# Attention beside a dense network: row maxima kept in queues of their own, more of them ahead of the loop, and slots joined in pairs

## The chip, the cores and the metric

The kernel runs on one core of one Trainium2 chip. The time is the device time of one execution in microseconds (us); several executions give a median and a span of values. One more execution is taken with the hardware profiler, and every instruction time below is from there.

## The reference

```python
xn = layernorm(x)                            # x: 2048 x 512, float32
qkv = xn @ wqkv                              # 32 heads of 16
p = softmax(q @ k.T * 16 ** -0.5)            # per head, 2048 x 2048
s = (p @ v) @ wo
h = relu(xn @ w1 + b1) ** 2                  # 2048 x 1792
g = silu(h @ w2 + b2)
out = x + s * g
```

All of it is float32. Products that need it are made from a high and a low part, three matmuls for one (`terms3`).

## The kernel before, in words

**Units and slots.** Attention is cut into 32 *units*: four heads (a *quad*) and 512 queries each, eight quads with four units. A unit has 16 *slots*, one for each block of 128 keys; there are 512 slots, numbered by `st`. In a slot four score matmuls with the keys on the output's partitions are made (`exp_mm`, L1125), one for each head, 64 rows of the array by 512 columns; ScalarE takes the exponential of each (L1132) into an SBUF tile. Two slots later four matmuls add these tiles, times V, to the unit's sums (`pv_mm`, L362, called a *PV* here; each shows as two records, so a PV is eight).

**Maxima.** The softmax needs the row maxima of a unit before its first slot. They come from score matmuls the other way round, queries on the partitions (`max_mm`, L289), 64 for each unit, 2048 in all, each followed by a VectorE reduction (L296). `max_mm(g, j)` serves unit `g // 16`; `g` is the slot plus `LEAD` = 24, so a unit's maxima end nine slots ahead of it. 24 such steps, 96 maxima, run ahead of the loop. `max_end` (L300) issues loads of K and Q at fixed steps of a unit and reduces the unit's maxima at its end; `shift` (L324) transposes and negates them and sends them through DRAM into two rows of the Q tile.

**Lanes and steps.** The array is split into two row tiles of 64, two *lanes*, that work at once. A *step* is one matmul on each lane. The scores of heads 0 and 2 of a quad and half of their maxima are on lane 0, the others on lane 1. The dense network and the output projection (WO) are cut in halves the same way: each accumulation first runs its upper half of rows on lane 0, later its lower half on lane 1, into the one dense bank (`pd`).

**Slots with dense work.** `slot` puts dense matmuls on one lane (six, or nine and twelve in WO's part), and four exponentials and three or four maxima on the other, in an order written as a string of `s` and `m`. `long_slots` (L1207) takes a *block* of 12 dense pieces for both lanes and spreads it over four slots, that is over two *visits* of two slots: in the first, lane 0 has the dense pieces, in the second, lane 1. A visit has ten steps (`D` ten times beside `msmsmsmsms`), a PV, four steps (`DDss` beside `mmsm`), a PV. The relus that empty a block's bank (`post`) are issued after the second of these four steps. The first dense matmul of a lane has a written dependency on `last_use`, an instruction that reads a score of the other lane (L209, L243); `long_slots` sets it to the exponential of the lane's first `s` of the part `DDss`.

**What sets the order.** TensorE, ScalarE, VectorE, GpSimd and SP run in the loop in the order in which the program is written. `later(n, fn)` runs something n slots on, at `begin`.

**Banks.** Eight PSUM banks: three for exponentials (`pe`), three for maxima (`pm`), one dense (`pd`), one for PV (`pv`). Tiles of a pool are taken in turn, and a matmul waits until the tile's last reader is done.

**Ahead of the loop.** After the layer norm `pump(n)` emits n matmuls of the projections to Q, K and V (twelve for each tile). 83 of them come alone, then the 24 lead steps of two maxima, eight projections, two maxima, eight projections; the last twelve fall into the loop's slots 0 and 1.

Of the kernel before, what the change touches and what calls it, by code (L numbers as in the profile page):

```python
# [8 lines left out]
F32 = mybir.dt.float32  # L9
# [7 lines left out]
P = 128  # L17
# [10 lines left out]
LEAD = 24  # L28
# [3 lines left out]
NPT = 14  # L32
NVT = 7
# [6 lines left out]
def kernel(  # L40
# [55 lines left out]
    with ExitStack() as ph:  # L96
# [8 lines left out]
        turn = {"ka": 0, "qm": 0, "qe": 0, "pt": 0}  # L105
# [6 lines left out]
        def oldest_first(name):  # L112
            n = turn[name] % len(rot[name])
            rot[name] = rot[name][n:] + rot[name][:n]
            turn[name] = 0
# [162 lines left out]
        togo = {}  # L278

        def max_mm(g, j):  # L280
            u = g // 16
            qd = u // 4
            if u not in mxs:
                mxs[u] = sp.tile([P, 16, 4], F32, name="mx")
                for i in range(2):
                    togo[u, i] = [(p, qb, kc) for p in range(2) for qb in range(4) for kc in range(4)]
            p, qb, kc = togo[u, j].pop(0)
            ps = pm.tile([P, 512], F32, name="pm_t")
            nc.tensor.matmul(  # L289
                ps,  # L290
                qms[u][p][64 * j : 64 * j + 64, qb * P : (qb + 1) * P],
                kas[qd, p][64 * j : 64 * j + 64, kc * 512 : (kc + 1) * 512],
                start=True, stop=True,
            )
            c = (2 * p + j) * 4 + qb
            return nc.vector.tensor_reduce(  # L296
                mxs[u][:, c, kc : kc + 1], ps, axis=AX.X, op=ALU.max
            )

        def max_end(g):  # L300
            u, s = divmod(g, 16)
            if u >= NU:
                return
            qd, qc = divmod(u, 4)
            if qc == 2 and qd + 1 < NQ and s % 2 == 0:
                load_k(qd + 1, s // 2)
            if qc == 3 and qd + 1 < NQ and s % 2 == 0 and s < 8:
                load_k(qd + 1, 8 + s // 2)
            if s in (7, 8):
                load_q_pair(u, "qe", s - 7, qes.setdefault(u, []))  # L310
            if s in (9, 11) and u + 1 < NU:
                load_q_pair(u + 1, "qm", (s - 9) // 2, qms.setdefault(u + 1, []))
            if s == 15:
                assert not togo[u, 0] and not togo[u, 1]
                m4 = sp.tile([P, 16], F32, name="m4")
                nc.vector.tensor_reduce(m4, mxs[u], axis=AX.X, op=ALU.max)  # L316
                mxs[u] = m4
                late.append((g + 2, u))

        def shift_due(g):  # L320
            if late and late[0][0] <= g:
                shift(late.pop(0)[1])

        def shift(u):  # L324
            pt = pm.tile([P, 512], F32, name="pm_t")
            nc.tensor.transpose(pt[:16, :P], mxs[u], ident)  # L326
            sh = sp.tile([16, 2, P], F32R, name="sh", bufs=1)
            nc.vector.tensor_scalar(sh[:, 0], pt[:16, :P], -1.0, None, op0=ALU.mult)
            nc.vector.scalar_tensor_tensor(
                sh[:, 1], pt[:16, :P], -1.0, sh[:, 0].bitcast(F32),  # L330
                op0=ALU.mult, op1=ALU.subtract,
            )
            def keep():
                for i in range(2):
                    nc.sync.dma_start(
                        sh_d[u][:, i, :].rearrange("h (b n) -> h b n", n=P),
                        sh[:, i, :].bitcast(F32),
                    )

            def back():  # L340
                for p in range(2):
                    for i in range(2):
                        shift_rows(u, p, i)

            if in_loop:
                later(1, keep)
                later(2, back)
            else:
                keep()
                back()  # L350
# [63 lines left out]
        def mlp_tasks(mp):  # L414
# [127 lines left out]
            def second(c, tt):  # L542
# [30 lines left out]
                if c == NCK - 1 and tt:  # L573

                    for i, task in enumerate(halves(mms, (6,) * 7, post, 1)):
                        if i == 4:
                            oldest_first("pt")
                            rot["pt"][:] = [t for t in rot["pt"] if all(t is not x for x in rot["ex"])]
                        yield task
                    return  # L580
# [19 lines left out]
            for c in range(NCK):  # L600
                if c == 1:

                    oldest_first("pt")
                    rot["pt"][:0] = rot["ex"]
# [307 lines left out]

        def qk_tile(m, c, last=False):
            ps = pd.tile([P, 512], F32, name="pd_t") if last else pe.tile([P, 512], F32, name="se")
# [13 lines left out]
            if m % 4 == 0:  # L928
# [10 lines left out]
        def v_tile(c, tt):  # L939
            xT = xTs[c]  # L940
            ps = pe.tile([P, 512], F32, name="se")
# [12 lines left out]
            nc.sync.dma_start(v_d[:, c * 4 + tt, :], vt.rearrange("p h d -> p (h d)"))  # L954
            yield
# [48 lines left out]
        def pump(n):  # L1004
            for _ in range(n):
                while True:
                    todo = ahead or rest
                    if not todo:
                        return
# [72 lines left out]
        pump(83)  # L1082
        warm = const.tile([P, 1], F32, name="warm")
        nc.scalar.activation(warm, eps_t, AF.Exp)
        for g in range(LEAD):
            shift_due(g)
            for j in range(2):
                max_mm(g, j)
            pump(8)
            for j in range(2):  # L1090
                max_mm(g, j)
            pump(8)
            max_end(g)
            if g == 0:
                raw_r = [load_w("wv", 3 * P, ((D + P, 3 * P),))]
            if g == 3:
# [4 lines left out]
            if g == 12:  # L1101
                s1.close()
                ep = ph.enter_context(tc.tile_pool(name="ep", bufs=1))
                rot["pt"] = [ep.tile([P, 512], F32, name=f"pt{i}") for i in range(NPT)]
                pools["n"] = ph.enter_context(tc.tile_pool(name="np", bufs=1))
            if g == 16:
                load_v(0)
                nc.sync.dma_start(b1_t, b1.rearrange("(fo p) -> p fo", p=P), allow_slow_non_contiguous=True)
                nc.sync.dma_start(b2_t, b2[None, :].to_broadcast([P, D]))
            if g % 2 and g < 16:  # L1110
                c, i = divmod(g // 2, 2)
                nc.sync.dma_start(
                    xn_d[i, :, :, c * 512 : (c + 1) * 512], xTs[c][:, i].bitcast(F32)
                )
        first.close()

        def exp_mm(st, j, pts, spare):
# [12 lines left out]
            pts[j] = ring("pt")  # L1130
            assert all(t is not pts[j] for d in pts_all.values() if d is not pts for t in d.values()), (st, j)
# [4 lines left out]
        def pv_step(st, pts):  # L1136
# [3 lines left out]
            pv_mm(pos[0], u // 4, kb, pts)  # L1140
            if kb == NT - 1:
# [28 lines left out]
        pts_all = pts  # L1170

        def slot(st, mms, post, fill=0):
            g = st + LEAD
# [4 lines left out]
            spare = g >= NU * 16  # L1178
# [13 lines left out]
            for i in range(len(other)):  # L1192
                if i < len(own):
                    own[i]()
                if other[i] is not None:
                    follow = other[i]()
                    if i >= len(own) - 1 and use is None:
# [6 lines left out]
            if not fill:  # L1204
                max_end(g)

        def long_slots(st0, units, post):  # L1207


            g0 = st0 + LEAD  # L1210
# [7 lines left out]

            for h in range(2):
                own, other = units[h], 1 - h  # L1220
                for part, (mine, theirs) in enumerate((("D" * 10, "msmsmsmsms"), ("DDss", "mmsm"))):
                    st = st0 + 2 * h + part
                    if st > st0:
                        begin(st)
                    for i, ops in enumerate(zip(mine, theirs)):
                        for lane in (h, other) if part else (other, h):
                            o = ops[0] if lane == h else ops[1]
                            if o == "D":
                                own.pop(0)()
                            elif o == "m":  # L1230
                                max_mm(g0, lane)
                            else:
                                use = s(lane)
# [4 lines left out]
                    max_end(st + LEAD)  # L1238
                    shift_due(st + 1 + LEAD)
                    pv_step(st - 2, pts.pop(st - 2))  # L1240
            if post is not None:
# [19 lines left out]
        def begin(st):  # L1261
            now[0] = st
            if st % 64 == 48 and st // 64 + 1 < NQ:
                load_v(st // 64 + 1)
            run_waiting()

        done = 0
        for st_ in range(NU * 16):
# [3 lines left out]
            if st_ < 2:  # L1272
                slot(st_, [], None, 6)
                shift_due(st_ + 1 + LEAD)
# [5 lines left out]
            if st_ == 2:  # L1280

                for g in (LEAD, LEAD + 1):
                    max_end(g)
# [9 lines left out]
            shift_due(st_ + 1 + LEAD)  # L1293
# [32 lines left out]
```

## Time and profile before

| | us |
|---|---|
| median of three runs | 1685.78 |
| lowest and highest | 1684.11, 1688.55 |
| profiled execution, first to last instruction | 1684.0 |
| TensorE busy in it | 1655.3 |
| VectorE, ScalarE, GpSimd busy | 1349.0, 1192.2, 525.5 |

For the profiled execution the profile gives the span from first to last instruction and no other time of its own; the three runs around it lie 0.1 to 4.6 us above that span.

How to read it: PE is TensorE's matmuls, PEld its weight loads, DVE is VectorE, ACT ScalarE, POOL GpSimd, SP the engine that issues the DMAs. In a timeline a row has the start, the time that the row covers, the engine, the line and the operation, the tiles, and how many instructions were merged; in brackets stands the idle time ahead of it and what ended that. A matmul row is longer than the spacing of matmuls, since they are pipelined.

### The profile page before, as it was taken

What the parts mean: (1) busy time and instruction counts of PE and PEld (TensorE: products, weight loads), DVE (VectorE), ACT (ScalarE), POOL (GpSimd) and SP (SyncE); (2) the same over time, 40 slices, a digit from 0 to 9 for tenths busy, and PEclk for the clock granted to TensorE, in tenths of its full rate; (3) what the DMA queues carried; (4) which work ended last, traced back from release to release, by engine and by line L of the source; (5) the groups of instructions that cost most, each with busy time, mean ns of one, the idle gap of its engine ahead of it and who ended that gap; (6) DMA issues with size and microseconds to landing.
All of it is one profiled execution on the core that took longest, in us unless ns stands there. A gap on an engine that the chain in (4) does not pass through costs nothing.

```text
span 1684.0 us, 35391 instructions
## 1 busy us (share of the span) xinstructions
PE 1655.3 (98%) x13296; PEld 941.3 (56%) x13296; DVE 1349.0 (80%) x2296; ACT 1192.2 (71%) x2354; POOL 525.5 (31%) x544
## 2 busy tenths in 40 slices
PE   6999999999999999999999999999999999999998
PEld 5766565556545655565466456545655565555533
DVE  6255688888888888888888888888888888887632
ACT  7211477777777777777777777777777777776685
POOL 4335566522212321231133113311221233134333
PEclk9999999999999999999999999999999999999998
DMA  8648566434333333433333334323433352157444
GB/s 282 177 144 268 165 204 186 117 83 141 90 90 92 116 83 99 100 105 78 103 117 85 85 93 142 95 65 105 137 81 83 82 151 57 44 169 228 140 125 134
DMA packets 156723, 208.00 MB, mean 124 GB/s; under 512 B 51272, under 2 KB 71240, under 8 KB 155016
## 3 DMA queue, kind: packets, MB, share of 16 engines
q1 hardware_dynamic: 156552, 205.74, 42.2%
q8 instruction: 105, 1.72, 0.4%
q14 instruction: 66, 0.54, 0.1%
HBM read 149.30 MB, written 56.09 MB: 122 GB/s over the span
## 4 chain that ended last, share of the span: by engine, by line
PE 88%; issue 4%; DMA 3%; POOL 2%; SPq 1%; DVE 1%; ACT 0%; POOLq 0%; ACTq 0%
PE po L362 27%; PE pm_t L289 17%; PE pd_t L236 16%; PE se L1125 12%; PE pd_t L204 6%; PE se L916 5%; PE se L947 3%; POOL ts L740 1%; POOL ts L741 1%; DMA oc<-on_d 0%; PE pm_t L816 0%; PE pm_t L326 0%; DMA xt<-in_A_x_dram 0%; DMA xc<-xn_d 0%; DMA hl<-r_d 0%
## 5 line engine op out<-in xcount | busy, mean ns | idle before, releaser
L296 DVE TENSOR_REDUCE mx<-pm_t 128x1 f32<-128x512 f32 x2048 | 1275.2, 684 | 233.0 <-PE pm_t L289 139.7
L1132 ACT ACTIVATE pt<-se 128x512 f32<-128x512 f32 x1730 | 902.9, 611 | 254.7 <-PE se L1125 221.6
L289 PE MATMUL pm_t<-ka,qm 64*128 64x512 f32 x2048 | 797.1, 423 | 3.9 <-DVE mx L296 3.7
L1125 PE MATMUL se<-qe,ka 64*128 64x512 f32 x2000 | 685.9, 402 | 0.0
L362 PE MATMUL po<-pt,v 128*32 128x512 f32 x3556 | 544.3, 604 | 0.0
L289 PEld LDWEIGHTS pm_t<-ka,qm 64*128 64x128 f32 x2048 | 352.8, 184 | 279.5 <-DVE mx L296 252.2
L1125 PEld LDWEIGHTS se<-qe,ka 64*128 64x128 f32 x2000 | 339.5, 184 | 21.3 <-issue 5.5
L236 PEld LDWEIGHTS pd_t<-xc,w1s 64*128 64x128 f32 x2352 | 292.1, 187 | 82.3 <-issue 82.2
L236 PE MATMUL pd_t<-xc,w1s 64*128 64x256 f32 x2352 | 332.2, 288 | 0.0
L236 PE MATMUL pd_t<-w2t,hT 64*128 64x512 f32 x936 | 259.9, 410 | 0.0
L236 PEld LDWEIGHTS pd_t<-w2t,hT 64*128 64x128 f32 x936 | 156.0, 184 | 71.2 <-issue 65.4
L362 PE MATMUL po<-ex,v 128*32 128x512 f32 x540 | 192.3, 605 | 0.0
L1132 ACT ACTIVATE ex<-se 128x512 f32<-128x512 f32 x270 | 147.5, 614 | 36.6 <-PE se L1125 31.6
L536 POOL TENSOR_TENSOR r<-r 128x512 f32<-128x512 f32 x49 | 50.9, 1040 | 331.3 <-ACT r L533 331.3
L362 PEld LDWEIGHTS po<-pt,v 128*32 128x32 f32 x3556 | 79.9, 108 | 132.3 <-issue 111.6
L555 POOL TENSOR_TENSOR u<-u,b_t 128x512 f32<-128x512 f32 x16 | 20.5, 1284 | 307.5 <-ACT u L554 307.5
L204 PE MATMUL pd_t<-w2t,hT 64*128 64x512 f32 x408 | 105.6, 391 | 0.0
L400 POOL TENSOR_TENSOR ot<-ot,hl 128x512 f32<-128x512 f32 x31 | 39.8, 1284 | 185.5 <-DMA hl<-r_d 134.8
L204 PE MATMUL pd_t<-wot,oc 64*128 64x512 f32 x336 | 90.4, 405 | 2.4 <-DVE m L316 0.8
L204 PEld LDWEIGHTS pd_t<-wot,oc 64*128 64x128 f32 x336 | 58.6, 184 | 49.1 <-DVE mx L296 12.5
L204 PEld LDWEIGHTS pd_t<-w2t,hT 64*128 64x128 f32 x408 | 72.6, 184 | 8.9
L533 ACT ACTIVATE r<-pd_t,b_t 128x256 f32<-128x256 f32 x98 | 41.1, 470 | 50.1 <-PE pd_t L236 50.1
(111 smaller groups left out, 1110.4 us busy)
## 6 DMA issues: line engine op xcount, KB each, us to landing
w1s<-w_d SPq DMA_DIRECT2D x196, 256.0 KB
qm<-q_d SPq DMA_DIRECT2D x384, 32.0 KB
qe<-q_d SPq DMA_DIRECT2D x384, 32.0 KB
ka<-k_d SPq DMA_DIRECT2D x96, 128.0 KB
xn_d<-xT SPq DMA_DIRECT2D x8, 1024.0 KB
k_d<-hl SPq DMA_DIRECT2D x32, 256.0 KB
q_d<-hl SPq DMA_DIRECT2D x32, 256.0 KB
xc<-xn_d SPq DMA_DIRECT2D x16, 512.0 KB
```

What stands on the lines that cost most here:

```text
L204: mm = nc.tensor.matmul(out_, lh(r), rh(r), start=first_ and lane == 0, stop=last_ and lane == 1, skip_group_check=True,)
L236: mm = nc.tensor.matmul(out_, lh(r), rh(r), start=first_ and lane == 0, stop=last_ and lane == 1, skip_group_check=True,)
L289: nc.tensor.matmul(ps, qms[u][p][64 * j : 64 * j + 64, qb * P : (qb + 1) * P], kas[qd, p][64 * j : 64 * j + 64, kc * 512 : (kc + 1) * 512] ...
L296: return nc.vector.tensor_reduce(mxs[u][:, c, kc : kc + 1], ps, axis=AX.X, op=ALU.max)
L362: nc.tensor.matmul(po[32 * j : 32 * j + 32, :], vs[qd][:, (4 * kb + j) * VW : (4 * kb + j) * VW + 32], pts[j], start=(kb == 0), stop=(kb = ...
L400: nc.gpsimd.tensor_tensor(ot, ot, hl[:, 1].bitcast(F32), op=ALU.mult)
L533: nc.scalar.activation(r[:, i], ps[:, i * CW : (i + 1) * CW], AF.Relu, bias=b1_t[:, fo : fo + 1])
L536: nc.gpsimd.tensor_tensor(r, r, r, op=ALU.mult)
L916: nc.tensor.matmul(out_, lh(slice(0, P)), rh(slice(0, P)), start=first_, stop=last_)
L947: nc.tensor.matmul(out_, lh(slice(0, P)), rh(slice(0, P)), start=first_, stop=last_)
L1125: nc.tensor.matmul(se, kas[qd, j // 2][b : b + 64, kb * P : (kb + 1) * P], qes[u][j // 2][b : b + 64, :], start=True, stop=True,)
L1132: return nc.scalar.activation(pts[j], se, AF.Exp, scale=0.25)
```

## The change

- The maxima are two queues, one for each lane (`todo_m`), in the order of units; `max_mm(j)` takes the next of lane j whatever the slot. `m_ready` holds back those whose K is not yet there. `max_end` follows the count of maxima that are done.
- Ahead of the loop 60 projections come alone, then bursts of three pairs of maxima and twelve projections until one projection tile is left: 34 bursts, 204 maxima. In the bursts maxima use the banks of `pm` and `pe` in turn, projections those of `pd` and `pv`. All projections that follow use the copy on ScalarE and the split on GpSimd.
- K of the next quad is loaded in the first six slots of a quad (of quad 1 ahead of the loop), Q for the exponentials one unit ahead; the shift's rows come back 14 slots ahead of the unit.
- Tiles for exponentials come from a list of free ones (`free_pt`), put back after the PV that reads them.
- Slots with over eight dense pieces take a fifth maximum, with over eleven a sixth.
- A visit of `long_slots` is *fused* where enough maxima are ahead (`ahead_m`, with `SHIFT` = 8): one part of 14 steps, with seven maxima in place of eight, and both PVs behind it. Otherwise it runs in two parts as before; here too the order in a step, the place of `post` and the choice of `last_use` are those of the new helper `visit`.

```diff
+        def ahead_m(n, st):
+            wo0 = 16 * NU - 62
+            for u in range(n // 64, NU):
+                end = 16 * u - SHIFT
+                n_max = n + 4 * max(0, end - st)
+                n_max += max(0, min(end, wo0 + 32) - max(st, wo0))
+                if n_max < 64 * (u + 1):
+                    return False
+            return True
...
+            def visit(h, mine, theirs):
+                own, other, use = units[h], 1 - h, None
+                for i, ops in enumerate(zip(mine, theirs)):
+                    for lane in (other, h):
+                        o = ops[0] if lane == h else ops[1]
+                        if o == "D":
+                            own.pop(0)()
+                        elif o == "m":
+                            max_mm(lane)
+                        elif o == "s":
+                            use = s(lane)
+                            if lane == h and not own:
+                                last_use[0] = use
             for h in range(2):
-                own, other = units[h], 1 - h
-                for part, (mine, theirs) in enumerate((("D" * 10, "msmsmsmsms"), ("DDss", "mmsm"))):
-                    st = st0 + 2 * h + part
-                    if st > st0:
-                        begin(st)
-                    for i, ops in enumerate(zip(mine, theirs)):
-                        for lane in (h, other) if part else (other, h):
...
-                                if part and lane == h and i == 2:
-                                    last_use[0] = use
-                        if part and h and i == 1 and post is not None:
-                            post()
...
+                st = st0 + 2 * h
+                if st > st0:
+                    begin(st)
+                if ahead_m(sum(done_m) + 7, st + 2):
+                    visit(h, "s" + "D" * 12 + "s", ".mmsmssmsmssmm")
+                    if h and post is not None:
+                        post()
+                    begin(st + 1)
+                    max_end()
+                    shift_due()
+                    for kb in (st - 2, st - 1):
+                        pv_step(kb, pts.pop(kb))
+                else:
+                    visit(h, "D" * 10, "msmsmsmsms")
+                    max_end()
+                    shift_due()
+                    pv_step(st - 2, pts.pop(st - 2))
+                    begin(st + 1)
+                    visit(h, "DDss", "mmsm")
+                    if h and post is not None:
+                        post()
+                    max_end()
+                    shift_due()
+                    pv_step(st - 1, pts.pop(st - 1))
```

In `slot`, and ahead of the loop:

```diff
-            own = [lambda: max_mm(g, lane) for _ in range(k)] + mms
-            mx = [] if spare else [lambda: max_mm(g, 1 - lane) for _ in range(4 - k)]
-            order = {0: "smsmsmsm", 1: "smsmssm", 2: "smsssm", 4: "ssss"}[4 if spare else k]
+            own = [lambda: max_mm(lane) for _ in range(m_ready(lane, k))] + mms
+            n_m = 4 - k + (len(mms) > 8) + (len(mms) > 11)
+            mx = [lambda: max_mm(1 - lane) for _ in range(m_ready(1 - lane, n_m))]
+            order = ("ssss", "sssms", "smsssm", "smsmssm", "smsmsmsm", "msmsmsmsm", "msmsmsmsmm")[len(mx)]
...
-        pump(83)
+        pump(60, 1)
...
-        for g in range(LEAD):
-            shift_due(g)
-            for j in range(2):
-                max_mm(g, j)
-            pump(8)
-            for j in range(2):
-                max_mm(g, j)
-            pump(8)
-            max_end(g)
+        while len(rest) > 1:
+            now[0] = b - 100
+            shift_due()
+            for _ in range(3):
+                for j in range(2):
+                    max_mm(j, True)
+            pump(12, 1)
+            max_end()
```

More of the change, by code (lines that the diff above doesn't have):

```diff
@@ L27 @@
 NU = NQ * 4
-LEAD = 24
 CW = 256
@@ L32 @@
 NPT = 14
+SHIFT = 8
 NVT = 7
@@ L284, in max_mm @@
                 mxs[u] = sp.tile([P, 16, 4], F32, name="mx")
[L285 to L288, printed above, removed]
+            m_bank[0] += 1
+            if spread and m_bank[0] % 2:
+                ps = pe.tile([P, 512], F32, name="se")
+            else:
+                ps = pm.tile([P, 512], F32, name="pm_t")
             nc.tensor.matmul(
@@ L346, in shift @@
                 later(1, keep)
-                later(2, back)
+                later(max(2, 16 * u - 14 - now[0]), back)
             else:
                 keep()
-                back()
+                if u < 2:
+                    back()
+                else:
+                    waiting.append((16 * u - 14, back))
         in_loop = []
@@ L1114 @@
                 )
+            b += 1
+        m0[0] = sum(done_m)
+        assert (1, 1) in kas and "n" in pools and 0 in vs, (b, after_v)
         first.close()
@@ L1140, in pv_step @@
             pv_mm(pos[0], u // 4, kb, pts)
+            free_pt.extend(t for _, t in sorted(pts.items()) if all(t is not x for x in gone_pt))
             if kb == NT - 1:
```

165 lines of the change are left out of this document (91 added, 74 removed).

## The prediction

> **What bounds the kernel now.** Read first the busy times, the slices and the groups.
>
> ```profile
> PE 1655.3 (98%) x13296; PEld 941.3 (56%) x13296; DVE 1349.0 (80%) x2296; ACT 1192.2 (71%) x2354; POOL 525.5 (31%) x544
> ...
> PE   6999999999999999999999999999999999999998
> ...
> DVE  6255688888888888888888888888888888887632
> ACT  7211477777777777777777777777777777776685
> ...
> PEclk9999999999999999999999999999999999999998
> ...
> L296 DVE TENSOR_REDUCE mx<-pm_t 128x1 f32<-128x512 f32 x2048 | 1275.2, 684 | 233.0 <-PE pm_t L289 139.7
> L1132 ACT ACTIVATE pt<-se 128x512 f32<-128x512 f32 x1730 | 902.9, 611 | 254.7 <-PE se L1125 221.6
> ```
>
> TensorE is busy in every slice at full clock; VectorE and ScalarE idle mostly until a matmul delivers. So TensorE's order sets the pace, and the others count only where they release it. How a visit runs is read next, from TensorE's timeline (start, duration): one whole visit and the start of the next.
>
> ```profile
> 838.74 0.50 PE L289 MATMUL pm_t<-ka,qm 64*128 64x512 f32 x1
> ...
> 844.40 0.50 PE L289 MATMUL pm_t<-ka,qm 64*128 64x512 f32 x1
> ...
> 844.74 0.40 PE L1125 MATMUL se<-qe,ka 64*128 64x512 f32 x1
> ...
> 844.98 0.39 PE L289 MATMUL pm_t<-ka,qm 64*128 64x512 f32 x1
> ...
> 846.98 1.06 PE L362 MATMUL po<-pt,v 128*32 128x512 f32 x8
> ...
> 847.99 0.50 PE L289 MATMUL pm_t<-ka,qm 64*128 64x512 f32 x1
> ...
> 848.55 0.39 PE L1125 MATMUL se<-qe,ka 64*128 64x512 f32 x2
> ...
> 848.79 0.39 PE L1125 MATMUL se<-qe,ka 64*128 64x512 f32 x1
> 849.11 1.07 PE L362 MATMUL po<-pt,v 128*32 128x512 f32 x8
> 850.10 0.50 PE L289 MATMUL pm_t<-ka,qm 64*128 64x512 f32 x1
> ...
> 855.80 0.50 PE L289 MATMUL pm_t<-ka,qm 64*128 64x512 f32 x1
> ```
>
> A visit is ten steps, a PV, four steps, a PV. The first step after a PV lasts 0.34 us (844.40 to 844.74), a later one about 0.235; last step to PV is 0.32 (848.79 to 849.11), PV to step 1.00 (846.98 to 847.99, 849.11 to 850.10). A visit of the first dense layer takes 5.70 (850.10 to 855.80), one of the second 5.66 (838.74 to 844.40).
>
> What the other engines give back, from their timelines:
>
> ```profile
> 848.98 1.58 ACT L1132 ACTIVATE pt<-se 128x512 f32<-128x512 f32 x3 [0.74 <-PE se L1125]
> ...
> 854.46 0.84 ACT L533 ACTIVATE r<-pd_t,b_t 128x256 f32<-128x256 f32 x2 [0.97 <-PE pd_t L236]
> 855.19 1.57 ACT L1132 ACTIVATE pt<-se 128x512 f32<-128x512 f32 x3
> ```
>
> ```profile
> 844.94 3.08 DVE L296 TENSOR_REDUCE mx<-pm_t 128x1 f32<-128x512 f32 x5 [0.21 <-PE pd_t L236]
> ```
>
> An exponential starts 0.43 us after its matmul (848.55, 848.98); they follow each other every 0.485, (1.58 - 0.61) / 2, and each holds its bank 0.61. Maxima follow every 0.60, (3.08 - 0.684) / 4. In the trace of before the three exponentials end at 850.56, after the next visit began at 850.10: nothing there waits for the last of them. The relus of a block stand ahead of its last exponentials.
>
> **The change, part by part.** Every sum is against the profiled span, 1684.0 us; little lies around it, as the three runs give 1684.1 to 1688.6, median 1685.8.
>
> **Ahead of the loop.** 34 bursts take the place of 48 groups of one pair of maxima and eight projection matmuls.
>
> ```profile
> 62.90 2.96 PE L947 MATMUL se<-wa_t,xT 128*128 128x512 f32 x12
> 65.70 2.96 PE L916 MATMUL se<-xT,wa_t 128*128 128x512 f32 x12
> 68.59 0.50 PE L289 MATMUL pm_t<-ka,qm 64*128 64x512 f32 x2
> 69.03 2.13 PE L947 MATMUL se<-wa_t,xT 128*128 128x512 f32 x8
> 71.08 0.50 PE L289 MATMUL pm_t<-ka,qm 64*128 64x512 f32 x2
> ...
> 186.91 0.49 PE L289 MATMUL pm_t<-ka,qm 64*128 64x512 f32 x1
> ```
>
> A projection matmul costs 2.80 / 12 = 0.233, a group 2.49 (68.59 to 71.08), all 48 118.3 (68.59 to 186.91, so 2.46 each). A burst adds two pairs and four projections to a group: 2.46 + 2 x 0.235 + 4 x 0.233 = 3.86. VectorE needs 6 x 0.60 = 3.6 of that; over six banks it just keeps up. 34 x 3.86 = 131.3; the lead starts 23 projections earlier (60 for 83), 5.4. **+7.5**, and between +6 and +11 if VectorE slips at the row maxima of each unit.
>
> **Fused visits.** The lead starts at 204, a fused visit eats one maximum of it, and the condition needs 96 left: counting the slots, the first 108 of the 176 visits are fused (60 of the first layer, 48 of the second), up to slot 290, and none of the 68 after. The steps stay 14; two changes of tiling become one. What a second PV behind a PV costs shows at the kernel's end only:
>
> ```profile
> 1665.85 3.07 PE L362 MATMUL po<-pt,v 128*32 128x512 f32 x24
> ```
>
> ```profile
> 1666.73 0.61 PE L362 MATMUL po<-pt,v 128*32 128x512 f32 x4
> ```
>
> The second PV starts 0.88 later. At TensorE's pace a fused visit is 0.34 + 12 x 0.235 to its last step (3.16), 0.32, 1.00 and 0.88: 5.36 against 5.70, 0.34 saved, 37 us in all. But eight exponentials now lie in one run of 14 steps, at steps 0, 3, 5, 6, 8, 10, 11, 13, over three banks. The second one's matmul starts at 0.81, its ACT at 1.24; the fifth's ACT at 1.24 + 3 x 0.485 = 2.70 ends at 3.31. Only then has the eighth its bank, at 3.37 with 0.06 for the release (a row below), and the exposed load lengthens it by 0.11 (0.50 against 0.39 above): 3.48 against 3.16. VectorE says nearly the same: the first maximum's matmul is at 0.34, its reduce starts at 0.77, the fourth reduce ends at 0.77 + 1.80 + 0.68 = 3.25, and the seventh matmul needs that bank: 3.42 with release and load. So 0.3 of the 0.34 goes in waiting for banks; I take 0.05 saved a visit: **-5**. Ends: -37 (no bank wait) and +11 (0.1 a visit lost, should an ACT operation such as the tanh or the copy of a PV's sums, 0.6 each, stand ahead of the first exponentials). Nothing else covers this wait: TensorE's queue is in order, both lanes stand. The Trainium skill, TensorEngine Tiling (Array Packing), PSUM Bottleneck, says that tiling speeds up TensorE but not the emptying of PSUM; these rows agree, and by TensorE's rows alone the sum would be 32 us less.
>
> **Visits that are not fused.** Two details are moved in them. First, the lane's dependency (the first dense matmul of the next visit waits for an exponential of this lane) is now the lane's last exponential, the third of the four-step part, where it was its first. That one ends at 850.56; with the release 0.06 the next visit's dense matmul may go at 850.62, not 850.10: 0.52. Behind it everything on TensorE stands. Second, the relus are issued behind those exponentials instead of ahead. Relative to the visit's start they run from 6.04 (6.16 less the overlap of 0.12 that 854.46 + 0.84 against 855.19 shows) to 6.88; the only dense bank is free at 6.94, the next block wants it at 5.70: 1.24. Of the 68 visits 21 end with that emptying (19 relu pairs, and 2 single copies at 1.06), 44 are followed at once by a dense matmul (0.52), three by a slot with a maximum first (0.2): 23.6 + 2.1 + 22.9 + 0.6 = **+49**. In the fused visits the same two waits are covered, since the last exponential (ACT 4.1 to 4.7) and the relus (to 5.5) end before the next dense matmul at 5.7 + 0.3. Ends: 0, were neither felt, and +60, should a further ACT operation of 0.6 stand ahead of the waited-for one in half of the 34 blocks.
>
> **WO's slots.** Does a dense matmul wait like that? Here one does, for VectorE's last maximum:
>
> ```profile
> 1505.40 2.48 DVE L296 TENSOR_REDUCE mx<-pm_t 128x1 f32<-128x512 f32 x4 [0.93 <-PE pm_t L289]
> ```
>
> ```profile
> 1501.21 0.18 PEld L204 LDWEIGHTS pd_t<-wot,oc 64*128 64x128 f32 x1 [0.84 <-DVE sh L328]
> ...
> 1507.94 0.18 PEld L204 LDWEIGHTS pd_t<-wot,oc 64*128 64x128 f32 x1 [0.90 <-DVE mx L296]
> ```
>
> The fourth maximum ends at 1507.88, the load goes at 1507.94: released at the end, 0.06 later. Two slots took 6.73. With a fifth maximum the chain from first step to the next dense matmul is 0.54 + 3.08 + 0.06 = 3.68 against 3.37; 21 such slots, and I take the same for the 4 with six maxima: 25 x 0.31 = **+7.8** (0 to +8). The maxima run out near slot 481 instead of 487; two short slots then lose their maxima (2.88 to 2.24): **-1.3**.
>
> ```profile
> 1607.81 1.07 PE L362 MATMUL po<-pt,v 128*32 128x512 f32 x8
> 1610.69 1.07 PE L362 MATMUL po<-pt,v 128*32 128x512 f32 x8
> ...
> 1616.02 1.06 PE L362 MATMUL po<-pt,v 128*32 128x512 f32 x8
> 1618.26 1.06 PE L362 MATMUL po<-pt,v 128*32 128x512 f32 x8
> ```
>
> **At nothing:** the list of free exponential tiles (17, at most 16 held), K in six slots instead of 24 and Q a unit ahead: the same DMAs on SP's queue, behind matmuls already done; without that cover some us per quad of heads, +0 to +5.
>
> Sum: 7.5 - 5 + 49 + 7.8 - 1.3 = +58: **1742**.
>
> **Rivals.** (B) The banks come free in time and fused visits run at TensorE's pace: 32 less, 1710. For it: the trace has hardly a bank wait today. Against: today three and five exponentials are parted by a PV. (C) They cost 0.1 more than now: 1758. (D) Only one wait of the unfused visits is felt, say not the exponential's: 1719. (E) The other side: banks and dependencies are released when the read starts, 0.61 to 0.68 earlier, not at its end. Then fused visits save 37, the exponential's wait and WO's vanish, the relus' falls to 0.77: 7.5 - 37 + 15.5 - 1.3 = -15, 1669. It decides from 0.3 us on (-37 + 10 + 19.5 + 7.5 - 1.3, about 0). Against it stands the 0.06 at 1507.94. (F) The change fuses all 176 visits: no late relus, 176 x -0.05 + 7.5 + 7.8 - 1.3, 1689. Against it: the count above. (G) The waits cost clock: were the 14 steps after each of 21 relu waits run at half clock, 21 x 3.2 = 67 more, 1809. The Trainium skill, TensorE: Matmul & The Clock Gate, A second HAM failure mode: psum-queue depth-cycling, says that short idling between groups of matmuls can make the clock swing; here PEclk is 9 in every slice but the last, WO's waits among them.
>
> **How the numbers follow.** Forecast 0.61 (1728 to 1756), B 0.12, C 0.08, D 0.08, E 0.05, F 0.04, G 0.02. The range from 1708 to 1758 takes in B, D and half of C, and leaves 0.15 out. About 0.3% is what a measurement of this kernel can tell from no change: faster 0.05 (E), same 0.04 (F), slower 0.91.
>
> **What would show it.** Step 1: the loop's first slot starts at about 194.5 instead of 186.9. Step 2: fused visits 5.6 to 5.7 long, load weights waiting for ACT and VectorE at steps 11 to 13. Step 3: from slot 292 on, dense loads behind a PV that wait 0.5 for an exponential and 1.2 for a relu, blocks of 13.2 for 11.4. Step 4: WO's slots at 3.68. The forecast is wrong if fused visits take 5.4, or if unfused blocks stay at 11.4.

## The result, and the profile after

| | before | after |
|---|---|---|
| median, us | 1685.68 (beside these runs) | 1729.59 |
| lowest and highest of the runs after, us | | 1729.0, 1730.45 |
| profiled span, us | 1684.0 | 1727.5 |

The ratio is 1.0252, with a 95% interval of 1.0235 to 1.0269: slower by 43.9 us, inside the predicted range and 12 below the forecast of 1742.

The page after, answering to the busy times, the slices and the groups of before:

```profile
PE 1671.6 (97%) x13296; PEld 997.1 (58%) x13296; DVE 1340.1 (78%) x2294; ACT 1194.8 (69%) x2354; POOL 528.9 (31%) x548
...
PE   6999999999999999999999999999999999999997
...
DVE  6599988887787788778777877887788778888612
...
PEclk9999999999999999999999999999999999999999
...
L234 PEld LDWEIGHTS pd_t<-xc,w1s 64*128 64x128 f32 x2352 | 296.4, 187 | 25.4 <-ACT r L545 16.5
```

Shares and clock have hardly moved, and busy TensorE grows by 16.3 where the span grows by 43.5: the page says that something waits, not where. The last row gives the first hint: weight loads of the first dense layer stood idle for 25.4 us, 16.5 of them ended by a relu (`r`).

The stretches say where. The cuts are the starts of the PVs of slots 58, 290 and 434, then of 448 and 480; a row has the window, its length, busy time and count of PE, PEld, DVE, ACT and POOL, the granted clock, the DMA share and GB/s. Before:

```profile
366.60:1030.20 663.60, 663.60 (x5843) 370.51 (x5842) 587.37 (x985) 511.88 (x1021) 160.29 (x158) 1.00 0.37 100
1030.20:1441.20 411.00, 411.00 (x3619) 229.27 (x3617) 364.18 (x612) 316.24 (x631) 105.21 (x105) 1.00 0.36 97
1481.80:1594.30 112.50, 109.82 (x807) 61.82 (x807) 82.11 (x137) 75.83 (x148) 48.02 (x41) 1.00 0.61 182
```

After:

```profile
377.30:1023.50 646.20, 642.77 (x5725) 396.64 (x5723) 511.40 (x873) 508.68 (x1019) 159.93 (x158) 1.00 0.38 102
1023.50:1479.60 456.10, 439.60 (x3619) 246.67 (x3617) 369.96 (x612) 321.12 (x631) 105.14 (x105) 1.00 0.32 88
1520.20:1640.00 119.80, 111.03 (x823) 64.61 (x822) 94.09 (x159) 75.48 (x147) 47.97 (x41) 1.00 0.57 171
```

The stretch with the fused visits has become shorter by 17.4. The one with visits that are not fused has the same 3619 matmuls and takes 45.1 longer; here the loss lies. WO's slots take 7.3 longer. By the same cuts, and up to the last PV, against the terms of the forecast:

| stretch | measured, us | forecast |
|---|---|---|
| start to the first PV | +12.4 (195.37 to 207.72) | +7.5 |
| slots 0 to 58 | -1.7 | 0 |
| 58 to 290, fused visits | -17.4 | -5 |
| 290 to 434, visits not fused | +45.1 | +49 |
| 434 to 448 | 0.0 | 0 |
| 448 to 480, WO | +7.3 | +7.8 |
| 480 to the last PV | -2.0 | -1.3 |
| sum | +43.7 | +58 |

Behind the last PV the changed kernel is another 0.2 shorter, so the spans differ by 43.5.

**Visits that are not fused.** TensorE's weight loads in one block after, where a row in brackets shows the idle time and what ended it:

```profile
1203.96 0.18 PEld L300 LDWEIGHTS pm_t<-ka,qm 64*128 64x128 f32 x1 [0.84 <-DVE mx L308]
...
1204.45 0.18 PEld L234 LDWEIGHTS pd_t<-xc,w1s 64*128 64x128 f32 x1 [0.31 <-ACT pt L1167]
...
1210.15 0.18 PEld L300 LDWEIGHTS pm_t<-ka,qm 64*128 64x128 f32 x1 [0.84 <-DVE mx L308]
...
1211.36 0.18 PEld L234 LDWEIGHTS pd_t<-xc,w1s 64*128 64x128 f32 x1 [1.03 <-ACT r L545]
```

ScalarE beside it:

```profile
1203.32 1.08 ACT L1167 ACTIVATE pt<-se 128x512 f32<-128x512 f32 x2
...
1210.46 0.85 ACT L545 ACTIVATE r<-pd_t,b_t 128x256 f32<-128x256 f32 x2
```

Each visit begins with a maximum's load, and the other lane's dense load should go with it. At 1203.96 it goes 0.49 later, when the exponential that ended at 1204.40 has released it; at 1210.15 it goes 1.21 later, when the relus ended at 1211.31. Both came 0.05 after the end of the read, and forecast were 0.52 and 1.24.

**Fused visits.** TensorE's timeline of one, from its first step to the first step of the next:

```profile
406.89 0.49 PE L1161 MATMUL se<-qe,ka 64*128 64x512 f32 x1
406.89 0.50 PE L300 MATMUL pm_t<-ka,qm 64*128 64x512 f32 x1
...
407.47 0.39 PE L1161 MATMUL se<-qe,ka 64*128 64x512 f32 x1
...
409.60 0.50 PE L1161 MATMUL se<-qe,ka 64*128 64x512 f32 x1
...
410.19 0.40 PE L1161 MATMUL se<-qe,ka 64*128 64x512 f32 x1
410.52 1.47 PE L374 MATMUL po<-pt,v 128*32 128x512 f32 x9
...
412.37 0.49 PE L1161 MATMUL se<-qe,ka 64*128 64x512 f32 x1
```

5.48 us where the forecast had 5.65 and TensorE's own pace would be 5.36. The string of the other lane begins with an empty step, and the forecast let that lane stand through it. It does not: its first maximum starts at 406.89, together with the score of the lane with the dense work, so it runs a step ahead throughout. Its first score, the visit's second exponential, is at 0.58 and not at 0.81, and the last step comes at 3.30 (410.19) where the forecast had 3.48. The Trainium skill, TensorEngine Tiling (Array Packing), Key Properties, says that tiles work independently of each other; these two rows agree.

**Ahead of the loop** a burst takes 3.83 to 3.90, forecast 3.86. The bursts together took 134.7 and not 131.3: the first took 4.68, the three with a unit's transpose and the ones behind them 0.1 to 0.35 more each, and one took 5.42. This is TensorE in that one, and SP's queue ahead of it:

```profile
146.88 0.50 PE L300 MATMUL se<-ka,qm 64*128 64x512 f32 x1
...
148.12 0.47 PE L300 MATMUL se<-ka,qm 64*128 64x512 f32 x1 [0.74 <-DVE mx L308]
```

```profile
129.23 3.83 SPq L1137 DMA_DIRECT2D b_t<-in_B_b_dram  x1
133.11 2.44 SPq L1140 DMA_DIRECT2D b_t<-in_B_b_dram  x1
...
143.43 2.83 SPq L132 DMA_DIRECT2D qm<-q_d  x6
```

The second maximum waits, and the six loads of its Q were issued only from 143.43 on. Its row names VectorE's last maximum; the row of the same burst in `e8_again` (below) names the load of Q. Two bias loads had held SP's queue for 6.3 us.

### The profile page after: what moved, and what is told of

The parts are those of the page before. It is cut to its first block, busy times and chain, and to the rows that moved or that the text cites. A ratio compares the mean times of both kernels' runs of the same rounds, so it can differ in the third digit from the quotient of the medians.

```text
span 1727.5 us, 35413 instructions
## 1 busy us (share of the span) xinstructions
PE 1671.6 (97%) x13296; PEld 997.1 (58%) x13296; DVE 1340.1 (78%) x2294; ACT 1194.8 (69%) x2354; POOL 528.9 (31%) x548
## 4 chain that ended last, share of the span: by engine, by line
PE 84%; issue 4%; ACT 3%; POOL 2%; DVE 2%; DMA 2%; SPq 1%; POOLq 0%; ACTq 0%; DVEq 0%
PE po L374 24%; PE pd_t L234 17%; PE pm_t L300 14%; PE se L1161 12%; PE pd_t L202 6%; PE pd_t L936 2%; PE po L936 2%; DVE mx L308 2%; ACT pt L1167 2%; PE se L300 2%; PE se L967 1%; ACT r L545 1%; PE se L936 1%; PE po L967 1%; PE pd_t L967 1%
## 5 line engine op out<-in xcount | busy, mean ns | idle before, releaser
L308 DVE TENSOR_REDUCE mx<-pm_t 128x1 f32<-128x512 f32 x1946 | 1212.0, 682 | 266.0 <-PE pm_t L300 150.8
L1161 PE MATMUL se<-qe,ka 64*128 64x512 f32 x1988 | 764.7, 423 | 2.0 <-ACT ex L1167 1.0
L300 PE MATMUL pm_t<-ka,qm 64*128 64x512 f32 x1946 | 737.9, 416 | 3.7 <-DVE mx L308 3.3
L374 PE MATMUL po<-pt,v 128*32 128x512 f32 x3562 | 522.2, 602 | 0.0
L300 PEld LDWEIGHTS pm_t<-ka,qm 64*128 64x128 f32 x1946 | 341.4, 184 | 215.3 <-DVE mx L308 198.2
L1161 PEld LDWEIGHTS se<-qe,ka 64*128 64x128 f32 x1988 | 352.7, 184 | 128.0 <-ACT pt L1167 56.8
L234 PE MATMUL pd_t<-xc,w1s 64*128 64x256 f32 x2352 | 317.7, 285 | 12.4 <-ACT r L545 11.4
L234 PEld LDWEIGHTS pd_t<-xc,w1s 64*128 64x128 f32 x2352 | 296.4, 187 | 25.4 <-ACT r L545 16.5
L234 PE MATMUL pd_t<-w2t,hT 64*128 64x512 f32 x936 | 247.5, 402 | 3.1 <-ACT r L545 2.4
L374 PE MATMUL po<-ex,v 128*32 128x512 f32 x534 | 204.8, 601 | 0.0
L234 PEld LDWEIGHTS pd_t<-w2t,hT 64*128 64x128 f32 x936 | 164.1, 184 | 20.7 <-issue 4.8
L202 PE MATMUL pd_t<-w2t,hT 64*128 64x512 f32 x408 | 105.6, 391 | 0.3
L308 DVE TENSOR_REDUCE mx<-se 128x1 f32<-128x512 f32 x102 | 69.6, 683 | 15.5 <-PE se L300 8.0
```

The costliest lines, as they stand in the source:

```text
L202: mm = nc.tensor.matmul(out_, lh(r), rh(r), start=first_ and lane == 0, stop=last_ and lane == 1, skip_group_check=True,)
L234: mm = nc.tensor.matmul(out_, lh(r), rh(r), start=first_ and lane == 0, stop=last_ and lane == 1, skip_group_check=True,)
L300: nc.tensor.matmul(ps, qms[u][p][64 * j : 64 * j + 64, qb * P : (qb + 1) * P], kas[qd, p][64 * j : 64 * j + 64, kc * 512 : (kc + 1) * 512] ...
L308: return nc.vector.tensor_reduce(mxs[u][:, c, kc : kc + 1], ps, axis=AX.X, op=ALU.max)
L374: nc.tensor.matmul(po[32 * j : 32 * j + 32, :], vs[qd][:, (4 * kb + j) * VW : (4 * kb + j) * VW + 32], pts[j], start=(kb == 0), stop=(kb = ...
L1161: nc.tensor.matmul(se, kas[qd, j // 2][b : b + 64, kb * P : (kb + 1) * P], qes[u][j // 2][b : b + 64, :], start=True, stop=True,)
```

## The experiments

**The theory**: the loss is the two waits of the visits that are not fused, one through `last_use` and one through `post`; each costs its share by itself, and they add. Fusing is a gain, cut down by banks and by work at the head of ScalarE's queue. **The rivals**: the loss comes with the two queues of maxima (other banks, other neighbours in each step) and stays when the two details are put back; or one wait covers the other, so that putting back one alone brings nothing; or fusing itself costs.

Stage figures below are of each kernel's profiled execution against before, by the cuts above.

**One wait away.** `e1_use` lets the lane depend on its first exponential again:

```diff
-                            if lane == h and not own:
+                            if lane == h and not own and first:
                                 last_use[0] = use
+                                first = False
```

> Unfused visits: the dependency is again the lane's first exponential of the four-step part (second in ScalarE's order, ends 5.67 after the visit's start), the relus stay late. Theory (the wait for the last exponential costs 0.46 to 0.50 at 44 places): 1729.6 - 21 = 1708, the 3.00 and 3.06 us row parts back to 2.6. Rival (the loss after slot 290 is the new order of loads and maxima): no change, 1729.

Measured: 1713.38 beside 1686.91, ratio 1.0174 (1.0136 to 1.0212), 5 above what was expected. Slots 290 to 434: +27.8 for +45.1, so 17.3 came back and not 21; the other stretches stayed within 1 us.

**The other wait away.** `e2_post` issues the relus behind the second of the four steps:

```diff
-                    visit(h, "DDss", "mmsm")
+                    visit(h, "DD", "mm")
                     if h and post is not None:
                         post()
+                    visit(h, "ss", "sm")
```

> Unfused visits: the relus stand again behind the second step of the four-step part, the dependency stays late. Theory (the late emptying of the dense bank costs 1.2 at 19 places and 1.0 at 2): 1729.6 - 25 = 1705; but the exponentials now end 0.7 later in the visits with relus, which no dependency follows there. Rival: no change, 1729; or the wait only moves to the dependency, 1718.

Measured: 1706.95, ratio 1.0123 (1.0107 to 1.0138). Slots 290 to 434: +20.3, so 24.8 came back.

**Both away.** `e3_both` has both edits.

> Both undone in unfused visits. Theory: the slots 290 to 434 take 411 us again instead of 456, in all 1729.6 - 45 = 1684.5, level with before. If the two waits hid each other, the sum of the two single gains is more than this one; the theory says they add, since they stand at different places (after the first and after the second visit of a block).

Measured: 1689.68 (1686.93 to 1694.94), ratio 1.0024 (1.0013 to 1.0035), 5 above what was expected. Its profiled execution is the longest of its ten, 1694.94, and in it the clock fell ahead of the loop (last section); the two stretches here ran at full clock:

```profile
383.60:1029.50 645.90, 642.51 (x5726) 396.46 (x5727) 511.65 (x872) 508.55 (x1018) 160.26 (x158) 1.00 0.39 101
1029.50:1444.30 414.80, 412.71 (x3618) 231.84 (x3617) 364.38 (x612) 317.49 (x631) 105.68 (x105) 1.00 0.37 97
```

Its loads at a visit's start:

```profile
1197.14 0.18 PEld L300 LDWEIGHTS pm_t<-ka,qm 64*128 64x128 f32 x1 [0.84 <-DVE mx L308]
1197.15 0.18 PEld L234 LDWEIGHTS pd_t<-xc,w1s 64*128 64x128 f32 x1
```

The dense load goes with the maximum's, nothing waits, and 414.8 us against 411.0 are left of 456.1. The two edits bring 41.3 together; one by one they brought 17.3 and 24.8, which is 42.1. So the waits add, neither covers the other, and the queues are not the cause: they are all still there.

**The same two waits in the kernel before.** `b_late` takes nothing of the change but the two details, in all 88 blocks:

```diff
-                                if part and lane == h and i == 2:
+                                if part and lane == h:
                                     last_use[0] = use
-                        if part and h and i == 1 and post is not None:
-                            post()
+                    if part and h and post is not None:
+                        post()
```

> The kernel before, with nothing of the change but the two late releases, in all its 88 blocks. Theory by the rows of the kernel after (0.46 for the last exponential at 65 places, 1.2 for the relus at 49, 1.0 for the copy at 6): 30 + 59 + 6 = 95, and 22 more for the first layer's 49 inner transitions at 0.46 where these are counted apart: 1686 + 118 = 1804 at most, 1780 at least. Rival (the waits come from the change's other parts, and the kernel before hides them): under 1700.

Measured: 1809.28 beside 1685.79, ratio 1.0726 (1.0695 to 1.0758). The added time lies in slots 58 to 290 (+75.7, 54 blocks) and 290 to 434 (+47.5, 34 blocks) and nowhere else: 1.40 for a block in both, near the 1.33 (45.1 / 34) of the changed kernel. It came out 5 above the upper end of what was expected. One dense load of it:

```profile
1200.45 0.18 PEld L289 LDWEIGHTS pm_t<-ka,qm 64*128 64x128 f32 x1 [0.84 <-DVE mx L296]
...
1200.94 0.18 PEld L236 LDWEIGHTS pd_t<-w2t,hT 64*128 64x128 f32 x1 [0.31 <-ACT pt L1132]
```

It goes 0.49 behind the maximum's load, released by the last exponential, as in the changed kernel: the same wait without queues, bursts or pairs.

**No fusing.** `e4_never` is `e3_both` with `if False:` in place of the condition.

> Both undone, and no visit is fused. Theory (a fused visit saves 0.19 to 0.23, less the four visits with a late tanh): the 17 us of the slots 58 to 290 are lost, some 5 come back in WO's slots since the maxima run out 20 slots earlier: 1684.5 + 12 = 1697. Rival (fusing saves nothing, the 17 us come from the loads that moved): 1680 to 1685.

Measured: 1699.22, ratio 1.0072 (1.005 to 1.0095), 9.5 above `e3_both`. Slots 58 to 290: +0.7 for -17.7, so fusing is worth 18 us there. Half of that doesn't show in the total. A lead that is never used up empties the queues early: WO's slots hold 41 maxima and not 149, and take +0.8 for +8.2. (The two profiled executions lie only 6.2 apart, since the loop started late in that of `e3_both`, at 213.2 for 209.4 here.)

**The fifth and sixth maximum.** `e5_wo4` is `e3_both` with `n_m = 4 - k`.

> Both releases undone as in e3_both (1689.7), and no fifth or sixth maximum in WO's slots. Theory (VectorE's chain of five sets those slots): the 8 us of the slots 448 to 480 go, 2 come back in the tail, where the maxima then end later: 1684. Rival (those slots wait for ScalarE or for DMAs): 1689.

Measured: 1681.63 beside 1685.96, ratio 0.9975 (0.9961 to 0.9989). WO's stretch: +0.7 for +8.2; the end -0.2 for -2.2. VectorE in two of WO's slots of the changed kernel shows why, and the dense load between them:

```profile
1530.04 3.08 DVE L308 TENSOR_REDUCE mx<-pm_t 128x1 f32<-128x512 f32 x5 [0.26 <-PE pm_t L300]
1533.72 3.08 DVE L308 TENSOR_REDUCE mx<-pm_t 128x1 f32<-128x512 f32 x5 [0.60 <-PE pm_t L300]
```

```profile
1533.18 0.18 PEld L202 LDWEIGHTS pd_t<-wot,oc 64*128 64x128 f32 x1 [1.21 <-DVE mx L308]
```

Five maxima from slot to slot take 3.68, as forecast, and the next dense load waits for the last, which ended at 1533.12.

**A later gate.** Four fused visits of the changed kernel have a row part about 1 us too long. ScalarE and GpSimd in one of them:

```profile
529.54 0.63 ACT L572 ACTIVATE r<-u 128x512 f32<-128x512 f32 x1 [1.40 <-POOL u L567]
```

```profile
528.22 1.29 POOL L567 TENSOR_TENSOR u<-u,b_t 128x512 f32<-128x512 f32 x1 [25.68 <-ACT u L566]
```

The tanh stands at the head of ScalarE's queue before GpSimd has its input ready (at 529.51); ScalarE stands for 1.40, and the exponentials behind the tanh with it. `e6_gate` is `e3_both` with `later(3, gate)` for `later(2, gate)`.

> As e3_both, with the tanh of the second dense layer one slot later. Theory (in four fused visits the tanh stands at the head of ScalarE's queue and waits for GpSimd, 1.0 us each): 1689.7 - 4 = 1686; the four row parts of 4.56 to 4.76 us become 3.6 to 3.9. Rival (those visits wait for something else): no change.

Measured: 1684.79, ratio 0.9996 (0.9986 to 1.0006). Slots 58 to 290: -21.8 for -17.7, four visits of 1.0.

**Another order of the 14 steps.** `e7_alt` is `e3_both` with the string `.msmsmsmsmsmsm`.

> As e3_both, with maxima and scores in strict turn on the other lane of a fused visit. Theory (what is left of the bank wait hangs on when ScalarE gets its second exponential, then 0.34 after the visit's start instead of 0.58): row part 3.61 becomes 3.55, 108 x 0.06 = 6 less, 1683. Rival (VectorE's banks set it): maxima come later on average, so the row part stays or grows, 1690 to 1695.

Measured: 1683.47, ratio 0.9985 (0.9976 to 0.9994). The row part is 3.57 for 3.61, the stretch -21.2.

**Half of ScalarE's work in fused visits.** `e9_half` is `e3_both` with exponentials of 256 columns there.

> As e3_both, but in fused visits each exponential covers 256 of its 512 columns (the other half of the probabilities is left as it was, so part of the computation is left out). Theory (ScalarE's banks set the row part of 3.61): it falls to 3.54, where VectorE's banks take over. Rival (VectorE's banks set it already): it stays at 3.61. If neither engine sets it, 3.61 as well, and if TensorE's pace is reached, 3.48.

Measured, in one run: 1684.3. TensorE's first step of one of its visits, its last steps and the PV:

```profile
386.10 0.50 PE L1163 MATMUL se<-qe,ka 64*128 64x512 f32 x1
...
389.21 0.49 PE L300 MATMUL pm_t<-ka,qm 64*128 64x512 f32 x1
389.31 0.40 PE L1163 MATMUL se<-qe,ka 64*128 64x512 f32 x1
389.64 0.62 PE L374 MATMUL po<-ex,v 128*32 128x512 f32 x2
```

The row part is 3.54, 0.07 shorter, and still 0.06 above TensorE's own 3.48 (3.16 and 0.32). ScalarE's banks set a fused visit, then something close behind it: the exposed load in front of the last maximum at 389.21 (0.49 for 0.39) points to VectorE's banks, which no run here took away.

**All together.** `e8_all` has the edits of `e3_both`, `e5_wo4`, `e6_gate` and `e7_alt`.

> All three on top of e3_both. If the gains add: 1689.7 - 5.5 - 4 - 6 = 1674, faster than before (1686.9) by 0.7%. Rival: with the lead phase at +12 and only 108 visits fused nothing is left, 1684 to 1687.

Measured: 1680.71 (1675.91 to 1685.71, 12 runs) beside 1685.96, ratio 0.9968 (0.9956 to 0.9979), 7 above what was expected. Slots 58 to 290 gave -25.2 as the parts promised, but WO's stretch had +4.6 where `e5_wo4` had +0.7, and the runs spread over 10 us.

**The transposes and the bias loads.** `e10_shift` is `e8_all` with the transposes of a fused visit behind its double PV, and the two bias loads a few bursts later.

```diff
                     max_end()
-                    shift_due()
                     for kb in (st - 2, st - 1):
                         pv_step(kb, pts.pop(kb))
+                    shift_due()
...
+                if k == 14:
                     nc.sync.dma_start(
```

> As e8_all; in fused visits the transposes of the row maxima stand behind the double PV instead of ahead of it, and the two bias loads are issued ten bursts later. Theory (two terms of the loss that the forecast did not have: 0.29 us for each of some 14 transposes of fused visits, part of it a change of tiling, and 1.6 us in the burst that waits for Q behind the bias loads): fused visits with a transpose 5.55 instead of 5.75 us, the burst of 5.42 back to 3.85, in all 3 to 5 us less than e8_all on the same chip. Rival (a transpose behind the PV costs the same, and the burst waits for the stores): no difference.

`e8_again` is the kernel of `e8_all` once more, beside it.

> The same program as e8_all, beside e10_shift on one chip: 1680 within 2.

Measured: 1675.88 (1673.36 to 1680.1) and 1681.73 (1676.98 to 1686.44), both beside 1685.58: 0.9941 (0.9928 to 0.9954) and 0.9974 (0.9961 to 0.9986). The long burst is gone. In `e8_again`:

```profile
147.51 0.46 PE L300 MATMUL se<-ka,qm 64*128 64x512 f32 x1 [0.21 <-DMA qm<-q_d]
```

In `e10_shift`, where burst follows burst:

```profile
143.97 0.49 PE L300 MATMUL se<-ka,qm 64*128 64x512 f32 x1
...
147.81 0.49 PE L300 MATMUL se<-ka,qm 64*128 64x512 f32 x1
```

It is 3.84 there, against 4.82 with the wait. A fused visit with a transpose became 0.13 shorter in its row part, less than was expected. These two account for 2 to 3 us of the 5.9 between the medians. The rest is about what the clock of the runs gives: each run has its mean granted clock on record, its median is 0.997 in `e10_shift` and 0.995 in `e8_again`, and 0.002 of 1680 us is 3.4, an estimate from figures with three places.

Where the clock is lost the traces show. In the profiled execution of `e10_shift`, the longest of its five, VectorE, TensorE and the window behind them show:

```profile
1532.33 0.25 DVE L398 RECIPROCAL sm<-sm 128x16 f32<-128x16 f32 x1 [6.20 <-DMA sm<-ot]
```

```profile
1533.19 0.79 PE L300 MATMUL pm_t<-ka,qm 64*128 64x512 f32 x1 [4.58 <-DVE mx L308]
```

```profile
1532.50:1539.10 6.60, 5.91 (x25) 3.12 (x26) 4.16 (x8) 1.79 (x3) 0.00 (x0) 0.50 0.77 256
```

The reciprocal of a unit's sums stands at the head of VectorE's queue until its DMA lands, the maxima behind it wait, TensorE stands for 4.58, and the 6.6 us that follow run at 0.50 of the clock. In `e8_all` the reciprocal waited 5.01 and TensorE 3.38 at the same place, with 6.7 us at 0.50 behind; in `e8_again` 4.04 and 2.41, with 3.3 us at 0.50. The wait near this place was 2.77 before and 1.43 in the changed kernel, and their clock stayed at 1.00. So this wait and its clock account for WO's +4.6 in `e8_all`. The spread of 10 us goes with the clock too: the runs of `e8_all` go from 1675.91 at 0.998 to 1685.71 at 0.993, and 0.005 of 1680 us is 8.4 of the 9.8. That the same wait takes the clock in the runs that were not profiled is a reading; no run moved it.

## Why the prediction was right, and where its sizes were off

- **The visits that are not fused** decided the sign, as forecast: +45.1 for +49, by the two waits named, at 0.49 and 1.21 for 0.52 and 1.24. `e1_use`, `e2_post`, `e3_both` and `b_late` show it from both sides. By these rows 19 x 1.20 + 2 x 1.0 = 24.8 is the relus' share, and `e2_post` brought 24.8. The exponentials' is 44 x 0.47 = 20.7, and `e1_use` brought 17.3; the 3.4 that are missing are about the 3.8 that `e3_both` keeps. In its trace a four-step part with a transpose takes 1.49 and one without 1.13, 0.36 for what cost 0.2 before, and the forecast had put nothing there; for 9 such parts that is some 1.4 of it. This was not tried by itself, and the rest is open.
- **WO's slots**: +7.3 for +7.8, slots of 3.68, shown by `e5_wo4`. The end: -2.0 for -1.3.
- **Fused visits** were the term that was mis-sized, -17.4 for -5. The step that failed is "the second one's matmul starts at 0.81": the lanes were taken to go in step. It starts at 0.58, and a visit saves 0.23 in the first layer and 0.19 in the second, not 0.05: 60 x 0.23 + 48 x 0.19 = 23. Some 5.6 of that went back, 4 to the late tanh (`e6_gate`) and 1.8 to the visit of slot 132, whose row part takes 5.40 for 3.62: there VectorE's reciprocal waits 2.95 for its DMA (581.38; this is read, not tried). The reason given for the limit, that banks come free too late, holds (`e9_half`), but costs 0.11 and not 0.29 a visit.
- **Ahead of the loop**: +12.4 for +7.5. The burst itself was right. What was left out is the first burst's wait, the bursts with transposes and Q behind the bias loads (3.4 together), and a start 1.15 later than forecast (64.37 for 63.22). That is there already at the transposes of the second tile of x (10.71 for 9.72), well ahead of the lead, and it varies: `e8_again`, up to there the same program, has its first burst at 63.39. Why the tile comes late is open. It was put at +6 to +11, so the end of that range was too near.
- **Slots 0 to 58**, put at 0, gave -1.7. Before, VectorE's reciprocal waits 1.96 for its DMA in this stretch, after it does not; this is read, not tried.
- **The signs.** Blocks of 13.1 where both waits stand and WO's slots of 3.68 came as named. The loop's first slot came at 199.09 and not at 194.5, and fused visits of 5.48 lie below the named 5.6 to 5.7, nearer to the 5.4 at which the prediction called itself wrong: that term failed, though it did not decide the sign.
- **The rivals.** B (5.36 a visit, 1710) and C (5.80) enclose the 5.48 measured, and B is nearer. D falls with `e1_use` and `e2_post`. E, release at the start of a read, falls with the loads that go 0.05 after its end. F falls by the count: 108 visits are fused, and slots 290 to 434 show visits in two parts. G, a lower clock behind the waits, does not come: 1.00 over all of slots 290 to 434.

So the forecast was right in sign and cause. Its sum was 14 above the measured one: 12 too little saved by fusing, 4 too much for the waits and 3 in the small terms, less 5 too little ahead of the loop. That the last took back part of the others is luck.

Of the change itself, fusing is worth 18 us in its stretch, and the two late releases (45) and the longer part ahead of the loop (12) outweighed it. With these put back, four maxima in WO's slots, the later gate, the other string, and transposes and bias loads moved, the kernel takes 1675.88, 0.6% less than before.

## What to carry to other kernels

When a helper that issues work is written anew, compare for each release (a dependency, an emptying of a bank) behind which instructions of its engine's queue it now stands: moved behind the last of three exponentials that follow each other every 0.48, it made TensorE wait 0.49 and 1.21 us at each such place, and the page's shares hardly showed it. Look for it in the stretch with the old amount of work and a longer time, in the loads with idle time in brackets. And count a lane with an empty step as one that runs ahead, and look at what stands at the head of each in-order queue (a tanh, a reciprocal, a bias load) when the work around it gets faster than its input: a wait of TensorE of 1.8 us or more cost clock as well in most places here.

## What the runs showed of the hardware that was not expected

The clock did fall, where no rival had looked for it: in WO's slots (above), once in a fused visit, and at the start of the lead. In `e3_both` the first maxima ahead of the loop waited for K from DRAM:

```profile
65.59 0.46 PE L300 MATMUL se<-ka,qm 64*128 64x512 f32 x1 [0.73 <-DMA ka<-k_d]
68.05 0.76 PE L300 MATMUL pm_t<-ka,qm 64*128 64x512 f32 x1 [2.00 <-DMA ka<-k_d]
```

The windows around it, with the granted clock as the third number from the end:

```profile
65.50:69.60 4.10, 2.01 (x6) 1.04 (x7) 1.44 (x3) 1.27 (x2) 3.21 (x2) 0.73 1.04 146
69.60:74.60 5.00, 5.00 (x13) 3.74 (x12) 2.34 (x4) 0.00 (x1) 0.00 (x0) 0.54 0.94 316
74.60:80.00 5.40, 5.40 (x27) 3.54 (x27) 4.48 (x8) 1.20 (x2) 0.63 (x2) 1.00 0.20 77
```

After idle times of 0.73 and 2.00, the next 5 us ran at 0.54 of the clock, and the first PV came at 213.2. `e9_half` did the same (0.55, 213.4); the first PV of the other kernels with the change came at 206.9 to 209.4. In `e10_shift` one wait did it, in the visit of slot 132, of TensorE for VectorE:

```profile
579.31 0.50 PE L300 MATMUL pm_t<-ka,qm 64*128 64x512 f32 x1 [1.78 <-DVE mx L308]
```

```profile
580.10:583.40 3.30, 3.30 (x22) 2.14 (x26) 2.96 (x6) 2.63 (x6) 0.00 (x0) 0.50 0.98 260
```

`e9_half` has the same at its slot 132. Waits of 1.2 us behind each block left the clock at 1.00, and so did one of 1.65 in `e8_again` (slot 132) and one of 2.08 in `e5_wo4` (1537.23), so length alone does not decide. The Trainium skill, TensorE: Matmul & The Clock Gate, HAM oscillation — how this bites in real kernels, puts the limit at idle gaps of more than about 3.4 us; here two gaps of 2.7 together, with one pair of matmuls between them, were enough, and so was a single one of 1.78. The start of the lead is therefore worth a look in any version of this kernel: its K comes back from DRAM just in time, and a miss costs more than the wait.
